# A gated linear attention with a gated feed-forward layer: the queries' factor from one reciprocal in place of a second scan

## The chip, the cores and the metric

The kernel runs on one core of one Trainium2 chip. The core has five engines that run side by side and wait for each other by semaphores: TensorE (PE, matrix products into PSUM; its weight loads are listed as PEld), VectorE (DVE), ScalarE (ACT), GpSimd (POOL) and SyncE (SP, which here issues nearly all DMAs). The metric is the device time of one execution in microseconds (us); lower is better. "Before" is the median of three runs.

## What is computed

For each of 4 x 8 heads, a state of 48 x 48 is carried along 768 positions. Each position scales the state's rows by a gate, adds an outer product of key and value, and reads the state with the query. All heads' results, 384 numbers for each of 3072 tokens, go through a feed-forward layer of width 2048:

```python
f = 1.0 / (1.0 + np.exp(-f_logit))
for t in range(S):
    state = f[:, :, t, :, None] * state + np.einsum('bhd,bhe->bhde', k[:, :, t], v[:, :, t])
    y[:, :, t] = np.einsum('bhd,bhde->bhe', q[:, :, t], state)
...
h = x @ w_in
g = h * np.clip(h + 3.0, 0.0, 6.0) / 6.0
return g @ w_out
```

## The kernel before

**Units.** The sequence is cut in chunks of 128 positions, 6 for each of 4 batches: 24 units, taken chunk by chunk through all batches (`UNITS`, line 40). A unit holds all 8 heads of its batch: 112 rows (two heads of 48 rows, at rows 0 and 64), 4 pairs of heads side by side, 128 positions each, so 512 elements in a row. Instead of stepping through positions, a unit multiplies keys and queries by factors made of the gates, and forms all pairs of positions by matrix products.

**The factors.** Let f be the gates of a chunk. `back` (line 349) scans them from the chunk's end to its start and makes `suffix`: at place t the product of the gates from t to the end, with 1 behind the last one. The tile has 4 x 129 elements, and one reset column for each pair of heads keeps the pairs apart. `kmul` (361) multiplies the key at t by the suffix product from t+1 on. `end` (368) keeps the whole chunk's product, which `decay` (381) applies to the carried state and which a check at the end of the program looks at: where a chunk's product is too small, the program computes everything again by a slow path. The queries need the reciprocal of the same suffix products. Before the change they come from a second scan: `rend` (turn, line 365) takes the reciprocal of the whole chunk's product, 4 elements in a row, into the reset columns of a tile that is otherwise zero, and `fwd` (forward, 373) scans the gates forward from there, 516 elements, in place over the gates. `qmul` (376) multiplies the queries by the result, one element further on.

**The rest of a unit.** `load` (330), `loadq` (333) and `loadv` (338) bring gates, queries with keys, and values; `gate` (343) is the sigmoid on ACT. `tk` and `ktok` transpose the keys, `att` (413) forms the scores, `mask` (423) applies causality on VectorE, `kv` (447) the chunk's own contribution to the state, `carry0` and `carry1` (466, 473) add it to the decayed state, `qs` (480) and `av` (496) give the result, and `xh`, `ym`, `xl`, `hole` (522 to 538) write it as a high and a low part into `xts`, the input of the feed-forward layer.

**The feed-forward layer.** A group is one chunk of all 4 batches, 512 tokens. For each of 16 slices of the width: `mm1` (line 560, nine matmuls, as weights and data are split into high and low parts and three products are kept), `relu` (570, ACT), `g` (574, VectorE), `gh` (583, ACT, the high part of the product), `gl` (587, VectorE, the low part) and `mm2` (604, nine matmuls; the last three read the low part). `pair` and `single` are PSUM banks 0 to 3 and 4; `tg` has three buffers, `gg` two. In the program's first part the weights are also converted from their 64-bit form, slice by slice: `ld`, `z`, `cy`, `mid`, `lim`, `dif`, `top`, `high`, `low` (lines 244 to 293) on ACT, VectorE and POOL.

**Order.** The order of all steps is written out by hand in `ORDER` (line 51), one token for each step and unit or slice. Each engine takes its own instructions in exactly that order; `ON_POOL` (43) names the steps that go to POOL instead of VectorE, some of the `kmul`, `qmul` and `decay` among them. A late instruction therefore delays everything behind it on its engine. Gates and suffix tiles have two buffers each (line 199), so the gate load of a unit waits for the `qmul` two units earlier.

Of the kernel before, what the change touches and what calls it, by code (L numbers as in the profile page):

```python
# [60 lines left out]
mid.3 rend.4 kmul.4 lowi.2 hole.3 ld.5 wd.2~hole.3 ga.1 lim.3 dif.3 back.5 mm2a.0 mm1a.2.1 mm2a.1 end.4 lim.4 end.5  # L61
z.4 mm1b.0.2 mm1b.1.0 mm1b.2.3 relub.0 relua.2 relub.1 top.3 fwd.4 qmul.4 cy.5 high.3 kmul.5 gb.0 ga.2 gb.1 tk.4.4
ktok.4 z.5 mm2b.0 tk.5.0 mm2a.2 ld.6~relub.0 mid.4 dif.4 top.4 mid.5 low.3 rend.5 high.4 relub.2 ktok.5 lim.5 low.4
fwd.5 dif.5 mm1.3.2 mm2b.1 att.4.0 mm1.4.4 cy.6 lim.6 mid.6 top.5 dif.6 decay.5 gb.2 mm2b.2 loadv.4~cy.5 ld.7
# [3 lines left out]
gh.5 mid.8 top.7 rend.6 dif.8 top.8 high.7 low.7 gl.5 fwd.6 tk.6.2 ktok.6 cy.9 high.8 low.8 mid.9 mm1.6.3 mm1.7.2  # L68
# [3 lines left out]
top.11 gl.8 decay.7 mm2.7 tk.7.3 mm2.8 low.10 carry0.6 xl.5 load.8 lim.12 relu.9 g.9 rend.7 carry1.6 ktok.7 z.12 ld.13  # L72
ld.14 cy.13 gh.9 fwd.7 mid.12 dif.12 top.12 gl.9 mm1.10.4 qs.6.2 kv.7.0 carry0.7 av.6 qmul.7 z.13 relu.10 xh.6 xl.6
# [4 lines left out]
rend.8 kmul.8 g.13 gh.12 gate.9 gl.12 end.8 relu.15 gh.13 mm2.12 tk.8.0 gl.13 back.9 fwd.8 mm2.13 gh.14 relu.16 ktok.8  # L78
g.15 qmul.8 kv.8.0 att.8.2 load.10 gh.15 kmul.9 decay.8 gl.14 rend.9 mm2.14 gl.15 mask.8 carry0.8 g.16 carry1.8 lowo.0
lowo.2 mm2.15 mm1.17.4 mm1.18.0 mm1.19.1 gh.16 gate.10 outs.0 outs.2 outv.1 fwd.9 gl.16 mm2.16 od.0 tk.9.3 od.2  # L80
relu.17 od.1 back.10 relu.18 end.9 end.10 qmul.9 g.17 rend.10 fwd.10 gh.17 relu.19 ktok.9 g.19 g.18 lowo.1 mm1.20.4
# [12 lines left out]
carry1.13 back.15 mask.13 mm1.33.4 mm2.30 qs.13.0 kv.14.2 av.13 hole.12 rend.15 loadq.15 loadv.15 load.16 loadv.16  # L94
loadq.16 gl.31 fwd.15 end.15 decay.15 qmul.15 kmul.15 carry0.14 relu.33 g.33 carry1.14 mm2.31 xh.13 xl.13 mm1.34.2
mm1.35.1 tk.15.3 outs.3 gate.16 gh.32 gl.32 back.16 rend.16 od.3 relu.34 gh.33 relu.35 end.16 outs.5 g.34 ktok.15
mm1.36.4 g.35 outv.4 od.5 kmul.16 att.14.2 kv.15.0 gl.33 od.4 relu.36 g.36 carry0.15 carry1.15 mask.14 fwd.16 qmul.16
# [60 lines left out]
def gla_moe(ctx: ExitStack, tc: tile.TileContext, unit, w, outT):  # L158
    nc = tc.nc
# [71 lines left out]
    rend = const.tile([PR, NP, C + 1], F32, name="rend")  # L231
    nc.gpsimd.memset(rend, 0.0)
# [88 lines left out]
    def engine(op, i):  # L321
        return nc.gpsimd if f"{op}.{i}" in ON_POOL else nc.vector

    def prep(i):
# [4 lines left out]

        def load():  # L330
            nc.sync.dma_start(out=gates[i % 2], in_=fg[u])
# [26 lines left out]
        def parts_of(t, x):
            return t[:, x].rearrange("r n c o t -> r c (n o) t")

        def kmul():
            t = chunks[i]
            engine("kmul", i).tensor_tensor(parts_of(t, 1), parts_of(t, 1), split(sf[:, :, 1:C + 1]), op=ALU.mult)  # L363

        def turn():
            nc.vector.reciprocal(rend[:, :, 0], sf[:, :, 0])
# [4 lines left out]
        past = gt[:, :NP * (C + 1)]

        def forward():
            nc.vector.tensor_tensor_scan(past, past, flat(rend), 0.0, op0=ALU.mult, op1=ALU.add)  # L374

        def qmul():
            t = chunks[i]
            to = past.rearrange("r (p c) -> r p c", p=NP)[:, :, 1:]
            engine("qmul", i).tensor_tensor(parts_of(t, 0), parts_of(t, 0), split(to), op=ALU.mult)  # L379

        def decay():
            engine("decay", i).tensor_tensor(
                decayed[i % 2][:, :, 0:D], state[b],
                ends[:, i].unsqueeze(2).broadcast_to([PR, NP, D]), op=ALU.mult,
            )
# [534 lines left out]
```

## Time and profile before

| | |
|---|---|
| median of 3 runs | 500.14 us (499.82 to 503.69) |
| span of the profiled execution | 500.6 us |
| HBM read, written | 36.43 MB, 4.72 MB |
| `back`, 24 scans on VectorE (L350) | 31.4 us busy |
| `qmul` on POOL (L379), 13 | 16.5 us busy, mean 1272 ns |
| `qmul` on VectorE (L379), 11 | 8.7 us busy, mean 797 ns |
| `rend` memset on POOL (L232) | 0.5 us, once, at 2.6 us |

The profile is of one execution; its times run from the first to the last instruction. A row of a timeline has the start in us, the duration in us, engine, line, operation, output and inputs, shapes and a count; in brackets the time that the engine was idle just before, and what ended that wait. A row of the groups by line has the count, then busy time in us and the mean of one in ns, then idle time before. [...] The 40 digits of an engine are its busy share, in tenths, in 40 equal slices of the span.

### The profile page before, as it was taken

What the parts mean: (1) busy time and instruction counts of PE and PEld (TensorE: products, weight loads), DVE (VectorE), ACT (ScalarE), POOL (GpSimd) and SP (SyncE); (2) the same over time, 40 slices, a digit from 0 to 9 for tenths busy, and PEclk for the clock granted to TensorE, in tenths of its full rate; (3) what the DMA queues carried; (4) which work ended last, traced back from release to release, by engine and by line L of the source; (5) the groups of instructions that cost most, each with busy time, mean ns of one, the idle gap of its engine ahead of it and who ended that gap; (6) DMA issues with size and microseconds to landing.
All of it is one profiled execution on the core that took longest, in us unless ns stands there. A gap on an engine that the chain in (4) does not pass through costs nothing.

```text
span 500.6 us, 11481 instructions
## 1 busy us (share of the span) xinstructions
PE 487.3 (97%) x4958; PEld 391.3 (78%) x4958; DVE 295.0 (59%) x462; ACT 217.6 (43%) x372; POOL 53.0 (11%) x57
## 2 busy tenths in 40 slices
PE   8789999999999999999999999999999999999996
PEld 4478787787888888788888888887887888788885
DVE  5959999989675736757405576645542243333341
ACT  5769989754343315433305434224322232333331
POOL 2211512203200200210100010100100000000000
PEclk9979999999999999999999999999999999999998
DMA  8877766432320330523100143300200000100001
GB/s 283 265 232 246 240 223 205 138 136 86 101 82 2 113 96 1 190 73 126 51 0 3 58 131 95 105 8 2 99 26 9 24 2 0 64 0 1 0 1 69
DMA packets 18969, 44.91 MB, mean 90 GB/s; under 512 B 2528, under 2 KB 8544, under 8 KB 18912
## 3 DMA queue, kind: packets, MB, share of 16 engines
q1 hardware_dynamic: 18768, 43.98, 26.5%
q8 instruction: 41, 0.67, 0.5%
q14 instruction: 16, 0.13, 0.1%
q10 hardware_dynamic: 144, 0.13, 0.1%
HBM read 36.43 MB, written 4.72 MB: 82 GB/s over the span
## 4 chain that ended last, share of the span: by engine, by line
PE 82%; DVE 11%; DMA 3%; ACT 1%; issue 1%; POOL 1%; SPq 0%; DVEq 0%; ACTq 0%
PE o L604 35%; PE pair L560 25%; PE single L560 11%; PE pair L487 2%; PE pair L456 2%; PE pair L504 2%; PE pair L418 2%; DVE top L281 2%; DMA raw<-w 2%; DVE w L285 1%; DVE gates L374 1%; DVE weight L293 1%; PE pair L655 1%; PE single L655 1%; DMA v<-unit 1%
## 5 line engine op out<-in xcount | busy, mean ns | idle before, releaser
L604 PE MATMUL o<-gg,weight 128*128 128x512 f32 x693 | 173.2, 399 | 0.5 <-DVE gg L587 0.5
L604 PEld LDWEIGHTS o<-gg,weight 128*128 128x128 f32 x693 | 128.0, 188 | 32.0 <-DVE gg L587 1.8
L560 PE MATMUL pair<-xts,weight 128*128 128x512 f32 x576 | 141.9, 396 | 0.0
L560 PEld LDWEIGHTS pair<-xts,weight 128*128 128x128 f32 x576 | 107.1, 188 | 24.5 <-DVE weight L293 0.2
L587 DVE TENSOR_TENSOR gg<-tg,gg 128x512 fp32r<-128x512 f32 x77 | 52.9, 692 | 68.2 <-ACT gg L583 68.2
L583 ACT ACTIVATE gg<-tg 128x512 fp32r<-128x512 f32 x77 | 48.2, 629 | 91.5 <-PE o L604 75.0
L574 DVE SCALAR_TENSOR_TENSOR tg<-tg,pair 128x512 f32<-128x512 f32 x64 | 42.8, 683 | 56.5 <-ACT tg L570 56.4
L570 ACT ACTIVATE tg<-pair,half 128x512 f32<-128x512 f32 x64 | 43.4, 685 | 62.9 <-PE pair L560 55.9
L560 PE MATMUL single<-xts,weight 128*128 128x512 f32 x261 | 66.5, 399 | 0.0
L560 PEld LDWEIGHTS single<-xts,weight 128*128 128x128 f32 x261 | 48.2, 188 | 10.9
L374 DVE TENSOR_TENSOR_SCAN gates<-gates,rend 112x516 f32<-112x516 f32 x24 | 33.3, 1386 | 0.2
L350 DVE TENSOR_TENSOR_SCAN suffix<-gates,unit 112x516 f32<-112x516 f32 x24 | 31.4, 1309 | 2.8 <-ACT gates L344 2.8
L570 ACT ACTIVATE tg<-single,half 128x512 f32<-128x512 f32 x29 | 19.8, 682 | 28.0 <-PE single L560 24.9
L363 POOL TENSOR_TENSOR qkf<-qkf,suffix 112x512 f32<-112x512 f32 x13 | 18.2, 1400 | 99.0 <-DVE suffix L350 35.2
L523 ACT ACTIVATE xts<-pair 112x512 fp32r<-112x512 f32 x24 | 14.3, 595 | 28.7 <-PE pair L456 14.6
L574 DVE SCALAR_TENSOR_TENSOR tg<-tg,single 128x512 f32<-128x512 f32 x29 | 19.7, 680 | 10.4 <-ACT tg L570 10.3
L604 PE MATMUL o<-xts,weight 128*128 128x512 f32 x96 | 25.3, 397 | 0.6 <-ACT xts L583 0.6
L379 POOL TENSOR_TENSOR qkf<-qkf,gates 112x512 f32<-112x512 f32 x13 | 16.5, 1272 | 85.0 <-DVE gates L374 40.6
L425 DVE TENSOR_TENSOR a<-pair,causal 128x512 f32<-128x512 f32 x24 | 16.4, 685 | 13.1 <-PE pair L504 9.3
L604 PEld LDWEIGHTS o<-xts,weight 128*128 128x128 f32 x96 | 17.8, 188 | 5.4 <-ACT xts L583 1.0
L456 PE MATMUL pair<-v,ktok 64*48 64x48 f32 (+1 forms) x768 | 16.4, 218 | 4.5 <-DVE top L281 2.4
L536 DVE TENSOR_TENSOR xts<-pair,xts 112x512 fp32r<-112x512 f32 x19 | 13.1, 687 | 11.6 <-ACT xts L523 11.6
(92 smaller groups left out, 452.2 us busy)
## 6 DMA issues: line engine op xcount, KB each, us to landing
qkf<-unit SPq DMA_DIRECT2D x24, 512.0 KB, 4.2
raw<-w SPq DMA_DIRECT2D x16, 768.0 KB, 5.5
gates<-unit SPq DMA_DIRECT2D x24, 258.5 KB, 3.2
v<-unit SPq DMA_DIRECT2D x24, 200.0 KB, 4.3
outT<-os SPq DMA_DIRECT2D x17, 256.0 KB, 2.1
xts<-xts SPq DMA_DIRECT2D x48, 48.0 KB, 2.2
weight<-w SPq DMA_DIRECT2D x3, 192.0 KB, 3.6
outT<-os SPq DMA_DIRECT2D x1, 128.0 KB, 3.7
```

The source lines that it names most:

```text
L350: nc.vector.tensor_tensor_scan(flat(sf)[:, ::-1], gt[:, 1:][:, ::-1], flat(unit)[:, ::-1], 0.0, op0=ALU.mult, op1=ALU.add,)
L363: engine("kmul", i).tensor_tensor(parts_of(t, 1), parts_of(t, 1), split(sf[:, :, 1:C + 1]), op=ALU.mult)
L374: nc.vector.tensor_tensor_scan(past, past, flat(rend), 0.0, op0=ALU.mult, op1=ALU.add)
L379: engine("qmul", i).tensor_tensor(parts_of(t, 0), parts_of(t, 0), split(to), op=ALU.mult)
L425: nc.vector.tensor_tensor(d["a"].rearrange("r p e t -> r e p t"), d["at"], causal.unsqueeze(1).unsqueeze(1).broadcast_to([128, 2, NP, HC]) ...
L456: nc.tensor.matmul(d["kv"][r:r + m, odd, c, n], d["ktok"][rs, 2 * n + part, r:r + m], heads_of(vt[rs], part, n, e)[:, :D], start=(odd, e) ...
L560: nc.tensor.matmul(h, win(f, a, k), g["xt"][:, k, :g["n"] // C, b], start=i == 0, stop=i == 3 * KT - 1,)
L570: nc.scalar.activation(d["t"], d["h"], AF.Relu, bias=half, scale=1.0 / 6.0)
L574: nc.vector.scalar_tensor_tensor(d["t"], d["t"], 1.0, d["h"], op0=ALU.min, op1=ALU.mult)
L583: nc.scalar.activation(d["gg"][:, 0], d["t"], AF.Copy)
L587: engine("gl", f if g["name"] == "0" else NU).tensor_tensor(d["gg"][:, 1], d["t"], d["gg"][:, 0].bitcast(F32), op=ALU.subtract)
L604: nc.tensor.matmul(g["o"][m], wout(f, a, m), g[f]["gg"][:, b], start=f == 0 and i == 0, stop=f == NF - 1 and i == 2, skip_group_check=True,)
```

## The change

`rend`, `fwd`, the tile of reset columns and its memset are taken out. In their place stands one step, `inv`: VectorE's reciprocal of the suffix products from the second column on, 4 x 128 elements in a row, written over the gates. `qmul` reads the gates' own columns in place of those one further on. In `ORDER` each `rend` token is dropped and each `inv` token stands where `fwd` stood; all other tokens keep their order.

```diff
@@ ORDER
-load.0 gate.0 back.0 rend.0 loadq.0 load.1 ld.0 loadv.0~gate.0 kmul.0 fwd.0 qmul.0 gate.1 warm.17 tk.0.3 ktok.0 warm.6
-att.0.0 kv.0.2 cy.0 back.1 loadq.1 loadq.2~load.1 mid.0 load.2 kmul.1 mask.0 rend.1 fwd.1 lim.0 qmul.1 ld.1 z.0
+load.0 gate.0 back.0 loadq.0 load.1 ld.0 loadv.0~gate.0 kmul.0 inv.0 qmul.0 gate.1 warm.17 tk.0.3 ktok.0 warm.6
+att.0.0 kv.0.2 cy.0 back.1 loadq.1 loadq.2~load.1 mid.0 load.2 kmul.1 mask.0 inv.1 lim.0 qmul.1 ld.1 z.0
...
@@
-    rend = const.tile([PR, NP, C + 1], F32, name="rend")
-    nc.gpsimd.memset(rend, 0.0)
@@
-        def turn():
-            nc.vector.reciprocal(rend[:, :, 0], sf[:, :, 0])
-
         def end():
             nc.scalar.activation(ends[:, i], sf[:, :, 0], AF.Copy)
 
-        past = gt[:, :NP * (C + 1)]
-
-        def forward():
-            nc.vector.tensor_tensor_scan(past, past, flat(rend), 0.0, op0=ALU.mult, op1=ALU.add)
+        def inverse():
+            nc.vector.reciprocal(rows, sf[:, :, 1:C + 1])
 
         def qmul():
             t = chunks[i]
-            to = past.rearrange("r (p c) -> r p c", p=NP)[:, :, 1:]
-            engine("qmul", i).tensor_tensor(parts_of(t, 0), parts_of(t, 0), split(to), op=ALU.mult)
+            engine("qmul", i).tensor_tensor(parts_of(t, 0), parts_of(t, 0), split(rows), op=ALU.mult)
@@
-            "kmul": kmul, "rend": turn, "end": end, "fwd": forward,
+            "kmul": kmul, "end": end, "inv": inverse,
```

More of the change, by code (lines that the diff above doesn't have):

```diff
@@ L60 @@
 load.5 ld.4~carry0.3 hole.2~wd.0 wd.1 loadq.5 relua.0 high.2 cy.3 xh.3 ym.3 ga.0 relua.1 xl.3 back.4 gate.5 z.3 cy.4
[L61 to L64, printed above, removed]
+mid.3 kmul.4 lowi.2 hole.3 ld.5 wd.2~hole.3 ga.1 lim.3 dif.3 back.5 mm2a.0 mm1a.2.1 mm2a.1 end.4 lim.4 end.5
+z.4 mm1b.0.2 mm1b.1.0 mm1b.2.3 relub.0 relua.2 relub.1 top.3 inv.4 qmul.4 cy.5 high.3 kmul.5 gb.0 ga.2 gb.1 tk.4.4
+ktok.4 z.5 mm2b.0 tk.5.0 mm2a.2 ld.6~relub.0 mid.4 dif.4 top.4 mid.5 low.3 high.4 relub.2 ktok.5 lim.5 low.4
+inv.5 dif.5 mm1.3.2 mm2b.1 att.4.0 mm1.4.4 cy.6 lim.6 mid.6 top.5 dif.6 decay.5 gb.2 mm2b.2 loadv.4~cy.5 ld.7
 loadv.5~ld.6 loadq.6~loadv.4 z.6 relu.3 top.6 high.5 cy.7 z.7 relu.4 g.3 low.5 decay.4 qmul.5 mask.4 kv.4.2 kv.5.0 g.4
@@ L67 @@
 ld.10 loadq.7~z.8 gl.3 back.6 mid.7 low.6 lim.7 att.5.2 av.4 kmul.6 g.5 mask.5 dif.7 gl.4 mm2.3 mm2.4 end.6 lim.8 z.9
-gh.5 mid.8 top.7 rend.6 dif.8 top.8 high.7 low.7 gl.5 fwd.6 tk.6.2 ktok.6 cy.9 high.8 low.8 mid.9 mm1.6.3 mm1.7.2
+gh.5 mid.8 top.7 dif.8 top.8 high.7 low.7 gl.5 inv.6 tk.6.2 ktok.6 cy.9 high.8 low.8 mid.9 mm1.6.3 mm1.7.2
 mm1.8.4 load.7~ld.10 ld.11 loadv.6 qmul.6 xh.4 ym.4 z.10 relu.6 g.6 relu.7 gh.6 xl.4 gate.7 g.7 lim.9 mm2.5 qs.5.0
@@ L71 @@
 kmul.7 dif.10 low.9 top.10 high.10 loadv.7 hole.4 ld.12 end.7 cy.12 gh.8 mm1.9.2 mid.11 lim.11 gl.7 dif.11 decay.6
-top.11 gl.8 decay.7 mm2.7 tk.7.3 mm2.8 low.10 carry0.6 xl.5 load.8 lim.12 relu.9 g.9 rend.7 carry1.6 ktok.7 z.12 ld.13
-ld.14 cy.13 gh.9 fwd.7 mid.12 dif.12 top.12 gl.9 mm1.10.4 qs.6.2 kv.7.0 carry0.7 av.6 qmul.7 z.13 relu.10 xh.6 xl.6
+top.11 gl.8 decay.7 mm2.7 tk.7.3 mm2.8 low.10 carry0.6 xl.5 load.8 lim.12 relu.9 g.9 carry1.6 ktok.7 z.12 ld.13
+ld.14 cy.13 gh.9 inv.7 mid.12 dif.12 top.12 gl.9 mm1.10.4 qs.6.2 kv.7.0 carry0.7 av.6 qmul.7 z.13 relu.10 xh.6 xl.6
 carry1.7 mm2.9 att.7.2 qs.7.0 mid.13 g.10 high.11 cy.14 gate.8 low.11 gh.10 z.14 lim.14 high.12 hole.6 ld.15 load.9
@@ L77 @@
 lim.15 dif.15 top.15 low.14 mm2.11 high.15 relu.12 low.15 mm1.14.0 mm1.15.1 mm1.16.4 back.8 g.12 relu.13 relu.14 g.14
[L78 to L81, printed above, removed]
+kmul.8 g.13 gh.12 gate.9 gl.12 end.8 relu.15 gh.13 mm2.12 tk.8.0 gl.13 back.9 inv.8 mm2.13 gh.14 relu.16 ktok.8
@@ L82 @@
+g.15 qmul.8 kv.8.0 att.8.2 load.10 gh.15 kmul.9 decay.8 gl.14 mm2.14 gl.15 mask.8 carry0.8 g.16 carry1.8 lowo.0
+lowo.2 mm2.15 mm1.17.4 mm1.18.0 mm1.19.1 gh.16 gate.10 outs.0 outs.2 outv.1 inv.9 gl.16 mm2.16 od.0 tk.9.3 od.2
+relu.17 od.1 back.10 relu.18 end.9 end.10 qmul.9 g.17 inv.10 gh.17 relu.19 ktok.9 g.19 g.18 lowo.1 mm1.20.4
 qs.8.0 att.9.2 av.8 kmul.10 qmul.10 decay.9 decay.10 mask.9 gl.17 kv.9.0 mm2.17 tk.10.2 mm1.21.3 xh.8 gh.18 load.11
 loadq.11 load.12 loadv.10 gh.19 gl.18 carry0.9 carry1.9 gl.19 xl.8 mm2.18 ktok.10 gate.11 relu.20 relu.21 back.11 g.21
-g.20 qs.9.0 att.10.2 av.9 kv.10.0 mm2.19 mm1.22.4 gate.12 back.12 end.12 end.11 gh.20 rend.11 carry0.10 fwd.11 qmul.11
@@ L85 @@
-load.13 loadq.12 kmul.11 mask.10 gl.20 tk.11.2 mm2.20 loadv.11 xh.9 relu.22 rend.12 g.22 gh.21 ktok.11 gh.22 gl.21
-gl.22 decay.11 fwd.12 carry1.10 mm1.23.4 relu.23 g.23 kmul.12 gate.13 mm2.21 mm1.24.3 gh.23 relu.24 mm2.22 mm1.25.4
+g.20 qs.9.0 att.10.2 av.9 kv.10.0 mm2.19 mm1.22.4 gate.12 back.12 end.12 end.11 gh.20 carry0.10 inv.11 qmul.11
+load.13 loadq.12 kmul.11 mask.10 gl.20 tk.11.2 mm2.20 loadv.11 xh.9 relu.22 g.22 gh.21 ktok.11 gh.22 gl.21
+gl.22 decay.11 inv.12 carry1.10 mm1.23.4 relu.23 g.23 kmul.12 gate.13 mm2.21 mm1.24.3 gh.23 relu.24 mm2.22 mm1.25.4
@@ L87 @@
 qmul.12 gl.23 relu.25 xl.9 g.24 gh.24 qs.10.0 att.11.2 av.10 kv.11.0 xh.10 mask.11 back.13 carry0.11 xl.10 g.25
-rend.13 carry1.11 mm2.23 mm1.26.3 tk.12.2 mm1.27.4 ktok.12 relu.26 gl.24 fwd.13 g.26 qs.11.0 att.12.2 av.11 hole.10
+carry1.11 mm2.23 mm1.26.3 tk.12.2 mm1.27.4 ktok.12 relu.26 gl.24 inv.13 g.26 qs.11.0 att.12.2 av.11 hole.10
 load.14 loadv.12 kv.12.0 loadq.13 loadv.13 qmul.13 mask.12 decay.12 gh.25 xh.11 gate.14 relu.27 xl.11 back.14
-carry0.12 rend.14 carry1.12 gl.25 mm2.24 hole.11 hole.9 load.15 gh.26 fwd.14 gl.26 g.27 hole.8 loadv.14 loadq.14
+carry0.12 carry1.12 gl.25 mm2.24 hole.11 hole.9 load.15 gh.26 inv.14 gl.26 g.27 hole.8 loadv.14 loadq.14
@@ L93 @@
 tk.14.4 g.32 qs.12.0 att.13.2 av.12 kv.13.0 qmul.14 end.14 ktok.14 gate.15 xh.12 gh.31 decay.14 carry0.13 xl.12
[L94 to L97, printed above, removed]
+carry1.13 back.15 mask.13 mm1.33.4 mm2.30 qs.13.0 kv.14.2 av.13 hole.12 loadq.15 loadv.15 load.16 loadv.16
+loadq.16 gl.31 inv.15 end.15 decay.15 qmul.15 kmul.15 carry0.14 relu.33 g.33 carry1.14 mm2.31 xh.13 xl.13 mm1.34.2
+mm1.35.1 tk.15.3 outs.3 gate.16 gh.32 gl.32 back.16 od.3 relu.34 gh.33 relu.35 end.16 outs.5 g.34 ktok.15
+mm1.36.4 g.35 outv.4 od.5 kmul.16 att.14.2 kv.15.0 gl.33 od.4 relu.36 g.36 carry0.15 carry1.15 mask.14 inv.16 qmul.16
 mm2.32 mm2.33 tk.16.4 gh.34 gh.35 ktok.16 qs.14.2 att.15.0 av.14 kv.16.2 decay.16 gl.35 carry0.16 carry1.16 mask.15
```

17 lines of the change are left out of this document (8 added, 9 removed).

## The prediction, made before the changed kernel ran

> **What bounds the kernel now.** I read the page's head first, then the groups by line with the shapes kept apart, then busy time by stage, and then the timeline of single instructions around each of the 24 places of the new instruction.
>
> ```profile
> span 500.6 us, 11481 instructions
> PE 487.3 (97%) x4958; PEld 391.3 (78%) x4958; DVE 295.0 (59%) x462; ACT 217.6 (43%) x372; POOL 53.0 (11%) x57
> DVE  5959999989675736757405576645542243333341
> ...
> 20.00:34.30 14.30, 10.55 (x261) 8.78 (x256) 8.86 (x13) 8.70 (x19) 2.49 (x2) 0.76 0.83 270
> 34.30:91.00 56.70, 55.92 (x699) 45.67 (x698) 55.84 (x91) 49.55 (x76) 14.51 (x9) 1.00 0.62 211
> 91.00:135.00 44.00, 43.98 (x456) 34.95 (x457) 37.65 (x57) 22.64 (x39) 9.93 (x8) 1.00 0.35 112
> 135.00:360.00 225.00, 225.00 (x2385) 182.70 (x2384) 129.01 (x202) 80.39 (x148) 20.81 (x19) 1.00 0.22 70
> ```
>
> Over the whole span TensorE is the bound: 487.3 of 500.6 us. The stages differ, and the last four rows show it (their columns are the stretch, busy time of PE, weight loads, DVE, ACT, POOL, then the granted clock and the DMA). Up to 34.3 us nothing is full but the DMA (0.83). From 34.3 to 91 us VectorE is busy 55.84 of 56.70 us, and TensorE 55.92: both are full, and VectorE has no spare time. From 135 to 360 us it has 96 us to spare. So the price of a VectorE instruction depends on its place: in full before 91 us, and later only what the lead of TensorE's inputs does not cover.
>
> **The price of the new instruction.** Removed are 24 scans of 516 elements (L374), 24 reciprocals of 4 elements (L366) and one POOL memset at 2.6 us, which stands in front of nothing late. Added are 24 reciprocals of 512 elements. The 512-element one isn't in the trace; the 4-element one is.
>
> ```profile
> L374 DVE TENSOR_TENSOR_SCAN gates<-gates,rend 112x516 f32<-112x516 f32 x24 | 33.3, 1386 | 0.2
> L366 DVE RECIPROCAL rend<-suffix 112x4 f32<-112x4 f32 x24 | 4.2, 175 | 0.2
> L425 DVE TENSOR_TENSOR a<-pair,causal 128x512 f32<-128x512 f32 x24 | 16.4, 685 | 13.1 <-PE pair L504 9.3 <-ACT th L631 3.7
> L478 DVE TENSOR_TENSOR state<-pair,middle 112x192 f32<-112x192 f32 x16 | 5.5, 350 | 0.1
> ...
> 22.68 0.35 DVE L269 TENSOR_SCALAR top<-top 128x768 uint16<-128x768 uint16 x1
> 22.95 1.22 DVE L374 TENSOR_TENSOR_SCAN gates<-gates,rend 112x516 f32<-112x516 f32 x1
> 24.09 0.53 DVE L281 TENSOR_TENSOR top<-top,mid 128x768 int16<-128x768 uint16 x1
> ```
>
> From 192 to 512 elements a product grows by 335 ns, 1.05 ns an element, which leaves about 150 ns that every instruction has. A reciprocal of 4 takes 175 ns, 25 ns over that. Counted over four elements that is 6 ns each; counted over the three steps from the first to the last element it is 8.3 ns. For 512 elements that gives 3.3 to 4.4 us of duration. From start to start an undisturbed instruction takes some 0.08 us less than its duration (the scan at 22.95 lasts 1.22, the next starts after 1.14). I take 4.3 us from start to start, the count by steps, since the common 150 ns holds the first element already. The bounds are 4.5 us above, and below the 0.6 us of a 512-element product. What goes is 1.14 + 0.09, so a place costs 3.1 us more; where the scan was stretched beyond 1.22, that much less. Over 24 places it is at most 74 us of VectorE time.
>
> [...]
>
> The rest of the edit is cheap. qmul reads the same tile at another offset, 512 elements as before. The order of all other steps is kept, so nothing is moved past a queue; but everything behind an inv on VectorE comes 3.1 us later, and so do POOL's qmuls, attention's scores, and the gate load two units on, which waits on SP for qmul to free the gates tile.
>
> **Stage by stage.** Units 0 to 3, up to 34.3 us:
>
> ```profile
> 7.75 0.69 DVE L379 TENSOR_TENSOR qkf<-qkf,gates 112x512 f32<-112x512 f32 x1
> 8.47 0.33 SPq L331 DMA_DIRECT2D gates<-unit  x1
> ...
> 24.65 1.07 PE L456 MATMUL pair<-v,ktok 64*64 64x48 f32 x48 [2.40 <-DVE top L281]
> ...
> 27.82 0.36 DVE L276 TENSOR_SCALAR mid<-top 128x768 uint16<-128x768 uint16 x1 [1.61 <-ACT top L267]
> ...
> 34.31 0.69 DVE L425 TENSOR_TENSOR a<-pair,causal 128x512 f32<-128x512 f32 x1 [3.71 <-ACT th L631]
> ```
>
> The load at 8.47 us is issued when qmul.0 ends (8.44), so unit 0's 3.1 us delay the whole SP queue; unit 1's second gate load slides by 4 us in the same way. Against that, four places add 12.4 us to VectorE, but it idles 1.61 and 3.71 us here, and TensorE 2.40 us for a v load that is late by less than VectorE is. Walking the four units through by these rows, the step at 34.31 us comes about 4.5 us later. Bounds: 2 (the load alone) and 8 (12.4 less the larger idle times).
>
> Units 4 to 7, 34.3 to 91 us:
>
> ```profile
> 41.01 2.24 DVE L374 TENSOR_TENSOR_SCAN gates<-gates,rend 112x516 f32<-112x516 f32 x1
> ...
> 90.28 0.69 DVE L587 TENSOR_TENSOR gg<-tg,gg 128x512 fp32r<-128x512 f32 x1
> ...
> 91.02 0.97 PE L604 MATMUL o<-gg,weight 128*128 128x512 f32 x3 [0.49 <-DVE gg L587]
> ```
>
> Unit 4's scan was stretched by 1.0, so it costs 2.1, the other three 3.1 each: 11.4 us. The cover is the stage's idle VectorE time, 56.70 - 55.84 = 0.9. At 91.02 TensorE waits for VectorE already, so no lead is left there: +10.5 us.
>
> Units 8 to 10, to 135 us:
>
> ```profile
> 116.58 4.68 PE L604 MATMUL o<-gg,weight 128*128 128x512 f32 x18
> 117.46 0.68 DVE L587 TENSOR_TENSOR gg<-tg,gg 128x512 fp32r<-128x512 f32 x1
> ...
> 132.62 0.36 DVE L382 TENSOR_TENSOR decayed<-state,ends 112x192 f32<-112x192 f32 x1 [2.36 <-PE pair L487]
> 133.84 0.69 DVE L425 TENSOR_TENSOR a<-pair,causal 128x512 f32<-128x512 f32 x1 [0.86 <-PE pair L504]
> 134.45 0.68 DVE L587 TENSOR_TENSOR gg<-tg,gg 128x512 fp32r<-128x512 f32 x1
> ...
> 134.09 2.37 PE L604 MATMUL o<-gg,weight 128*128 128x512 f32 x9
> ...
> 138.95 2.11 PE o L604 x9
> ```
>
> A second matmul block (L604) takes 2.11 us, and reads the low half of gg in its last three of nine matmuls, 1.4 us after its start. At 116.58 two blocks take 4.68 instead of 4.22, held by the low half that ends at 118.14: no lead, so unit 8 costs 3.1. Units 9 and 10 add 6.2; VectorE's idle 2.36 and 0.86 take 3.2 of it, and the low half that ends at 135.13 has 0.4 us until 135.5: +2.6. Stage: +5.7 us.
>
> Units 11 to 23, after 135 us, where each delay meets idle VectorE time soon:
>
> ```profile
> 146.47 0.68 DVE L587 TENSOR_TENSOR gg<-tg,gg 128x512 fp32r<-128x512 f32 x1
> ...
> 147.61 2.34 PE L604 MATMUL o<-gg,weight 128*128 128x512 f32 x9
> ...
> 154.85 0.69 DVE L587 TENSOR_TENSOR gg<-tg,gg 128x512 fp32r<-128x512 f32 x1 [0.31 <-ACT gg L583]
> ...
> 156.07 2.26 PE L604 MATMUL o<-gg,weight 128*128 128x512 f32 x9
> ...
> 233.87 0.69 DVE L587 TENSOR_TENSOR gg<-tg,gg 128x512 fp32r<-128x512 f32 x1 [2.38 <-ACT gg L583]
> 239.30 0.67 DVE L574 SCALAR_TENSOR_TENSOR tg<-tg,pair 128x512 f32<-128x512 f32 x1
> ...
> 241.07 2.34 PE L560 MATMUL pair<-xts,weight 128*128 128x512 f32 x9
> ...
> 299.16 1.82 DVE L374 TENSOR_TENSOR_SCAN gates<-gates,rend 112x516 f32<-112x516 f32 x1
> 302.36 0.67 DVE L574 SCALAR_TENSOR_TENSOR tg<-tg,pair 128x512 f32<-128x512 f32 x1
> ...
> 305.09 0.36 PE L437 MATMUL pair<-ident,qkf 112*128 112x112 f32 x2
> ```
>
> Unit 11: the low half ends at 147.15 and is needed at 149.0, a lead of 1.9, so 1.2 is lost. Unit 12: 3.1 - 0.31 idle - 1.9 lead = 0.9. Units 17 and 18 stand close together: 3.1 - 2.38 + 3.1 = 3.8 late at 239.30, whose bank (0) the block at 241.07 overwrites 1.1 us after it is read: 2.7. Units 19 and 20: 3.1 + 2.5 (that scan took 0.6 more than 1.22) = 5.6 at 302.36; the transposes of unit 20 want the same bank 2.05 us after it: 3.5. The others meet idle times of 2 us and more, or a lead of about 3; I give them 0.6 together. Stage: +8.9 us, between 4 (leads twice as long) and 18.
>
> One thing more: the clock. The row from 20 to 34.3 us has a granted clock of 0.76 after TensorE's one long idle time (2.40 us), which is 0.24 x 14.3 = 3.4 us of TensorE work. The new stalls of 2.7, 3.1 and 3.5 us are as long. Before 135 us such a loss mostly runs beside VectorE's own lateness; I count one in full: +3.4, bounds 0 and 10.
>
> [...]
>
> **Sum:** 4.5 + 10.5 + 5.7 + 8.9 + 3.4 = 33.0 us on the span of 500.6, which is 0.5 above the median of 500.14: 533 us. Its own range, from the bounds of the terms, is 515 to 553.
>
> **Rivals.** (1) Later delays aren't absorbed. ACT runs relu and the high halves in one order, so a late product can hold the relu behind it, and the lead of two gg buffers is used up at each place. Then all 13 late units cost 3.1: 500 + 4.5 + 10.5 + 9.3 + 40.3 = 565 us. It decides once a delay outlasts the next relu. Against it:
>
> ```profile
> ACT gg L583 <- PE o L604: 75.0, 35, 11.9
> ```
>
> ACT waits 75 us in 35 places for TensorE, which is lead to give away. [...] (3) Not slower: the 25 ns are a fixed start-up of the reciprocal, and elements then stream like a product's, 0.6 us each. VectorE then gains 0.6 in each place. Only the seven places between 34.3 and 135 us where it holds TensorE count: 500 - 4 = 496 us. It decides if the instruction takes under 1.2 us. The 25 ns allow it, but then every other kind of instruction's 150 ns would not hold for this one.
>
> **How the numbers follow.** Forecast 0.70, rival 1 0.12, rival 2 0.12, rival 3 0.06. The range runs from rival 2's 504 to 556, where the forecast's range ends with some room, and leaves out rivals 1 and 3: 0.18. A measurement tells about 1%, 5 us, from no change: faster takes a sixth of rival 3, 0.01; same the rest of it and some of rival 2, 0.08; slower 0.91.
>
> **What will show it.** [...] VectorE's busy time should rise by about 70 us to 365. The step that stood at 91.02 us should come near 106; the last block before 135 us near 156. After that TensorE's waits on VectorE should lie at units 11, 12, 17/18 and 19/20, not at every unit; if they lie at all 13, rival 1 holds. The clock row should show one or two more stretches at half speed.

## The result, and the profile after

The changed kernel takes 516.54 us (median of 4 runs, 513.95 to 517.27) against 501.91 us (4 runs, 499.82 to 505.34): a ratio of 1.0292 [1.0252, 1.0332]. It is slower, as forecast, but the loss of some 15 us is less than half of the 33 us that the sum gave. A span is some 1.7 us shorter than the time of the same run. The profiled execution has a span of 515.6 us, 15.0 more than the 500.6 of before. In the changed kernel's profile the lines have moved: the new reciprocal is L366, `qmul` L370, `kmul` L360, `mask` L416, `tk` L428, `g` L565, `gl` L578, `mm1` L551, `mm2` L595.

The head of the page and its costliest groups, changed kernel:

```profile
span 515.6 us, 11453 instructions
...
PE 491.7 (95%) x4958; PEld 393.7 (76%) x4958; DVE 337.6 (65%) x438; ACT 218.1 (42%) x372; POOL 51.0 (10%) x56
...
DVE  6999999988978784877823369746852343333342
...
L366 DVE RECIPROCAL gates<-suffix 112x512 f32<-112x512 f32 x24 | 80.2, 3341 | 0.0
L347 DVE TENSOR_TENSOR_SCAN suffix<-gates,unit 112x516 f32<-112x516 f32 x24 | 30.9, 1289 | 2.8 <-ACT gates L341 2.8
```

The new instruction takes 3.34 us each time, not 4.4. VectorE's busy time rises by 42.6 us (295.0 to 337.6), not by 70. The groups account for it: 80.2 came, the scans' 33.3 and the small reciprocals' 4.2 went, and that makes 42.7. The digits of VectorE at the left end have risen from "59599999" to "69999999": the holes that it had in the first stage are filled.

Busy time by stage, changed kernel (columns as before: the stretch, PE, weight loads, DVE, ACT, POOL, then the granted clock and the DMA):

```profile
0.00:20.00 20.00, 16.77 (x250) 9.30 (x250) 15.53 (x17) 11.35 (x19) 4.80 (x18) 0.83 0.74 259
20.00:34.30 14.30, 11.09 (x292) 8.47 (x285) 14.27 (x15) 9.82 (x22) 1.58 (x3) 0.88 0.73 241
34.30:91.00 56.70, 52.77 (x587) 42.83 (x588) 55.00 (x80) 45.54 (x71) 13.68 (x9) 0.97 0.62 209
91.00:135.00 44.00, 40.70 (x402) 31.84 (x401) 40.40 (x52) 23.30 (x37) 6.87 (x5) 0.96 0.34 114
135.00:360.00 225.00, 220.47 (x2380) 178.78 (x2379) 151.03 (x185) 78.65 (x145) 22.35 (x21) 1.00 0.22 70
```

From 20 to 34.3 us VectorE was busy for 8.86 us and now is for 14.27: the stage swallowed the new work. From 34.3 to 135 us TensorE was busy for 99.9 of 100.7 us and now for 93.5. There the loss shows.

To see where the time goes, I take four instructions of VectorE that both kernels have, one at the end of each stage, and subtract their starts. Each start is a row of the two timelines. In the changed kernel the first, third and fourth are:

```profile
34.37 0.68 DVE L416 TENSOR_TENSOR a<-pair,causal 128x512 f32<-128x512 f32 x1
...
145.85 0.68 DVE L578 TENSOR_TENSOR gg<-tg,gg 128x512 fp32r<-128x512 f32 x1
...
375.39 0.69 DVE L659 COPY os<-o 128x512 f32<-128x512 f32 x1 [0.53 <-PE o L595]
```

The last of them in the old kernel:

```profile
360.04 0.69 DVE L668 COPY os<-o 128x512 f32<-128x512 f32 x1 [2.67 <-PE o L604]
```

| VectorE instruction | start before, us | later by, us | added in the stage, us |
|---|---|---|---|
| `mask.3` | 34.31 | 0.06 | 0.06 |
| `gl` ahead of the block at 91.02 | 90.28 | 7.95 | 7.9 |
| last `gl` ahead of 135 us | 134.45 | 11.40 | 3.45 |
| first copy of the last outputs | 360.04 | 15.35 | 3.95 |

One trace of the old kernel is not a sharp ruler. Two kernels of the next section have the same instructions up to `mask.3` and start it at 32.79 and 31.77 us. So the change adds 0.1 to 2.6 us in the first stage, and the 0.06 of the table is the lower end. From there on the second of them stays 1.9 us ahead of this trace (88.33 and 132.59 us for the next two rows).

The `gl` that stood at 90.28 us, and the block that waits for it, in the timeline of the changed kernel:

```profile
92.20 3.33 DVE L366 RECIPROCAL gates<-suffix 112x512 f32<-112x512 f32 x1
...
95.46 0.28 DVE L273 TENSOR_SCALAR mid<-top 128x768 uint16<-128x768 uint16 x1
...
98.23 0.68 DVE L578 TENSOR_TENSOR gg<-tg,gg 128x512 fp32r<-128x512 f32 x1
...
98.96 0.96 PE L595 MATMUL o<-gg,weight 128*128 128x512 f32 x3 [2.43 <-DVE gg L578]
```

From the reciprocal's start to the next instruction's are 95.46 - 92.20 = 3.26 us. The scan and the small reciprocal that went took 1.14 + 0.09 = 1.23, so a place costs 2.03 us more, not 3.1. The block that stood at 91.02 stands at 98.96, and its wait has grown from 0.49 to 2.43 us.

TensorE's longest waits, changed kernel (us in total, times, longest):

```profile
PE pair L409 <- DVE qkf L370: 3.9, 2, 2.1
PE o L595 <- DVE gg L578: 3.5, 2, 2.4
PE pair L428 <- DVE a L416: 1.3, 1, 1.3
PE pair L478 <- ACT xts L525: 1.2, 1, 1.2
PE o L631 <- DVE th L626: 1.2, 1, 1.2
...
PE single L551 <- DVE weight L290: 0.8, 1, 0.8
PE pair L447 <- DVE tg L565: 0.8, 1, 0.8
...
PE pair L551 <- DVE tg L565: 0.8, 1, 0.8
```

The two waits of the first row are attention's scores of units 0 and 2 behind `qmul`. They stand in the first stage, whose end isn't late in these two traces. The third row is new, and the prediction did not name it:

```profile
154.76 3.34 DVE L366 RECIPROCAL gates<-suffix 112x512 f32<-112x512 f32 x1
158.13 0.69 DVE L370 TENSOR_TENSOR qkf<-qkf,gates 112x512 f32<-112x512 f32 x1
158.74 0.68 DVE L360 TENSOR_TENSOR qkf<-qkf,suffix 112x512 f32<-112x512 f32 x1
...
159.34 0.68 DVE L416 TENSOR_TENSOR a<-pair,causal 128x512 f32<-128x512 f32 x1
...
160.09 0.60 PE L428 MATMUL pair<-ident,qkf 112*128 112x112 f32 x4 [1.29 <-DVE a L416]
```

This is unit 11. Its `kmul` and the mask of unit 10 stand behind `inv` and `qmul` on VectorE. The transposes of unit 11's keys (L428) need both: the keys, which `kmul` has ready at 159.42 us, and PSUM bank 2, where unit 10's scores stay until the mask has read them at 160.02 (`att.10.2` and `tk.11.2` in `ORDER`). The mask ends last, and TensorE waits 1.29 us for it, before the product that the prediction looked at.

### The profile page after: what moved, and what is told of

It reads as the page before. It is cut to its first block, busy times and chain, and to the rows that moved or that the text cites. A ratio compares the mean times of both kernels' runs of the same rounds, so it can differ in the third digit from the quotient of the medians.

```text
span 515.6 us, 11453 instructions
## 1 busy us (share of the span) xinstructions
PE 491.7 (95%) x4958; PEld 393.7 (76%) x4958; DVE 337.6 (65%) x438; ACT 218.1 (42%) x372; POOL 51.0 (10%) x56
## 4 chain that ended last, share of the span: by engine, by line
PE 64%; DVE 8%; ACT 1%; issue 1%; DMA 1%; ACTq 0%
PE o L595 28%; PE pair L551 20%; PE single L551 7%; DVE gates L366 4%; PE pair L478 2%; PE pair L409 2%; PE pair L495 1%; PE pair L646 1%; PE single L646 1%; DVE suffix L347 1%; PE pair L447 1%; DVE tg L565 1%; DMA gates<-unit 1%; PE pair L428 1%; DVE qkf L360 0%
## 5 line engine op out<-in xcount | busy, mean ns | idle before, releaser
L595 PE MATMUL o<-gg,weight 128*128 128x512 f32 x693 | 170.9, 396 | 3.5 <-DVE gg L578 3.5
L595 PEld LDWEIGHTS o<-gg,weight 128*128 128x128 f32 x693 | 127.9, 188 | 33.1 <-DVE gg L578 4.9
L551 PE MATMUL pair<-xts,weight 128*128 128x512 f32 x576 | 142.4, 397 | 1.2 <-DVE tg L565 0.8
L551 PEld LDWEIGHTS pair<-xts,weight 128*128 128x128 f32 x576 | 106.9, 188 | 26.7 <-DVE tg L565 1.0
L578 DVE TENSOR_TENSOR gg<-tg,gg 128x512 fp32r<-128x512 f32 x77 | 53.4, 698 | 57.0 <-ACT gg L574 56.9
L574 ACT ACTIVATE gg<-tg 128x512 fp32r<-128x512 f32 x77 | 48.3, 629 | 99.9 <-PE o L595 74.4
L366 DVE RECIPROCAL gates<-suffix 112x512 f32<-112x512 f32 x24 | 80.2, 3341 | 0.0
L565 DVE SCALAR_TENSOR_TENSOR tg<-tg,pair 128x512 f32<-128x512 f32 x64 | 42.4, 680 | 52.3 <-ACT tg L561 52.1
L551 PE MATMUL single<-xts,weight 128*128 128x512 f32 x261 | 68.0, 404 | 0.9 <-DVE weight L290 0.8
L551 PEld LDWEIGHTS single<-xts,weight 128*128 128x128 f32 x261 | 48.7, 191 | 12.7 <-DVE weight L290 1.3
L360 POOL TENSOR_TENSOR qkf<-qkf,suffix 112x512 f32<-112x512 f32 x13 | 17.2, 1326 | 100.7 <-DVE suffix L347 68.9
L370 POOL TENSOR_TENSOR qkf<-qkf,gates 112x512 f32<-112x512 f32 x13 | 16.7, 1288 | 99.8 <-DVE gates L366 59.5
L565 DVE SCALAR_TENSOR_TENSOR tg<-tg,single 128x512 f32<-128x512 f32 x29 | 19.7, 679 | 10.4 <-ACT tg L561 10.4
L595 PE MATMUL o<-xts,weight 128*128 128x512 f32 x96 | 25.4, 397 | 0.6 <-ACT xts L574 0.6
L595 PEld LDWEIGHTS o<-xts,weight 128*128 128x128 f32 x96 | 17.8, 188 | 5.5 <-ACT xts L574 1.0
L416 DVE TENSOR_TENSOR a<-pair,causal 128x512 f32<-128x512 f32 x24 | 16.3, 681 | 7.2 <-PE pair L495 6.6
L527 DVE TENSOR_TENSOR xts<-pair,xts 112x512 fp32r<-112x512 f32 x19 | 13.0, 684 | 11.5 <-ACT xts L514 11.5
L409 PE MATMUL pair<-qkf 48*64 48x64 f32 x768 | 16.5, 222 | 3.9 <-DVE qkf L370 3.9
```

What stands on the lines that cost most here:

```text
L366: nc.vector.reciprocal(rows, sf[:, :, 1:C + 1])
L409: nc.tensor.matmul(d["at"][HC * odd:HC * (odd + 1), e, 2 * n + c], t[rs, 1, n, c, odd], t[rs, 0, n, c, odd], start=True, stop=True,)
L416: nc.vector.tensor_tensor(d["a"].rearrange("r p e t -> r e p t"), d["at"], causal.unsqueeze(1).unsqueeze(1).broadcast_to([128, 2, NP, HC]) ...
L551: nc.tensor.matmul(h, win(f, a, k), g["xt"][:, k, :g["n"] // C, b], start=i == 0, stop=i == 3 * KT - 1,)
L565: nc.vector.scalar_tensor_tensor(d["t"], d["t"], 1.0, d["h"], op0=ALU.min, op1=ALU.mult)
L574: nc.scalar.activation(d["gg"][:, 0], d["t"], AF.Copy)
```

## The experiments

Three questions were open: whether the stages really lose what the lag table says, or the loss comes from interplay; whether the forecast's walk through the stages was right and its price alone wrong; and what the half clock, which shows in the windows above (0.83, 0.88), costs. All kernels use the changed kernel's or the old kernel's text with one edit. The kernels of the first two groups were compared with the old kernel on the same chip, at a median of 500.95 us (17 runs) for the first four and of 501.25 us (6 runs) for the next four; the last two with 502.22 us (17 runs).

**The reciprocal in some units alone.** Three kernels keep the second scan except in one range of units:

```diff
+            if i in [0, 1, 2, 3]:
+                to = rows
...
-warm.1 ym.1 mask.2 kmul.3 rend.3 lowi.0 lim.1 fwd.3 dif.1 qmul.3
+warm.1 ym.1 mask.2 kmul.3 lowi.0 lim.1 inv.3 dif.1 qmul.3
```

> The reciprocal in units 0 to 3 alone, the scan in the other 20. Theory A (up to 34 us the loads' landing sets the end, so VectorE's extra 2.0 us a place is absorbed): 0 to +1.5 us on before, and the mask of unit 3 starts within 1 us of its 34.3 us in before. Theory B (a delay of the first units is carried to the end, and the trace of the full change hides it behind a lucky clock): +3 to +6 us.

> The reciprocal in units 4 to 10 alone. Theory A (VectorE has no idle time from 34 to 130 us, so each place costs its 2.0 us nearly in full): +10 to +13 us on before, most of the full change's loss. Theory B (the loss is spread evenly over the 24 places, 0.6 us each): +4 us.

> The reciprocal in units 11 to 23 alone. Theory A (VectorE's idle time absorbs most): +2 to +5 us on before, in two or three places, at units 11/12 and where two inv stand close together (19 and 20). Theory B (evenly spread): +8 us.

| reciprocal in units | median, us | ratio | span, us |
|---|---|---|---|
| 0 to 3 | 503.28 (10 runs) | 1.0046 [1.0020, 1.0071] | 502.0 |
| 4 to 10 | 511.92 (4 runs) | 1.0225 [1.0165, 1.0286] | 510.7 |
| 11 to 23 | 506.08 (8 runs) | 1.0113 [1.0081, 1.0144] | 503.3 |

By medians these are +2.3, +11.0 and +5.1 us. The second lies where theory A put it and the third at A's upper end of 5; B's 4 and 8 us lie outside their intervals. The first lies between A and B, with an interval from 1.0 to 3.6 us: a part of what the first four places delay does come out later. Its trace shows that only in part (its `mask.3` is 0.14 us late, its `gl` of the old 90.28 us 1.68), as the old trace's own `mask.3` is 1.5 and 2.5 us later than those of the second and third kernel. The three sum to 18.4 us and the full change has about 15; with the widths of the four intervals this difference isn't clear of noise. The third kernel, with no reciprocal before unit 11, has the same new wait of the transposes in its waits of TensorE:

```profile
PE pair L442 <- DVE a L430: 1.3, 1, 1.3
```

**The price, set by idle work.** Three kernels keep the scan and add, between it and `qmul`, memsets of columns that are zero already. They hold up VectorE as a longer reciprocal would, at a price that their number sets. They don't hold up the 13 `qmul` that run on GpSimd, which wait for the scan alone: that of unit 6 starts 1.36 us behind the start of the scan, without memsets and with three, and 3.43 us behind the start of the reciprocal.

```diff
+        def pad():
+            for _ in range(4):
+                nc.vector.memset(rend[:, :, 1:], 0.0)
```

> The kernel before with four VectorE memsets of 512 zeros behind each fwd, in the zero part of the reset tile (some 0.5 us each by the 516-element one of before, so about 2.0 us more a place, as the reciprocal). Theory A (VectorE's time alone counts): the time of the full change within 3 us, 512 to 518 us. Theory C (something of the reciprocal itself costs: how it reads, or who waits for its result): well below that, under 508 us.

> The scan with three memsets of 512 zeros behind it. Four of them took 2.52 us from start to start instead of the 2.0 expected (each waits for the one ahead, 0.66 us apiece), so three cost 1.86 us a place, a little less than the reciprocal's 2.03. Theory A (only VectorE's time a place counts): 9 to 14 us on before, a little under the full change. Theory C (the reciprocal is special, and memsets cost more for the same time): 18 us or more, three quarters of what four memsets cost.

> The scan with five memsets behind it: 3.18 us a place, the price that the prediction gave the reciprocal (3.1). Theory P (the walk through the stages was right and only the price was wrong): the predicted 33 us on before, between 29 and 40. Theory Q (the walk overstates by itself: the loss is proportional to the price, as 15 us at 2.03 say): 23 to 25 us.

The first rows of the timeline of the kernel with five, at unit 0, show what price that makes:

```profile
6.49 1.23 DVE L374 TENSOR_TENSOR_SCAN gates<-gates,rend 112x516 f32<-112x516 f32 x1
7.89 0.48 DVE L378 MEMSET rend<- 112x512 f32 x1 [0.17 <-DVE gates L374]
8.55 0.48 DVE L378 MEMSET rend<- 112x512 f32 x1 [0.17 <-DVE rend L378]
...
10.93 0.63 DVE L383 TENSOR_TENSOR qkf<-qkf,gates 112x512 f32<-112x512 f32 x1
```

`qmul` starts 4.44 us after the scan instead of 1.26 (6.49 to 7.75 before): 3.18 us a place, the price that the prediction had assumed. Memsets of one tile wait for each other, 0.66 us from start to start. So four of them cost 2.52 us (more than the 4 x 0.485 of their durations), and three 1.86. That is why the kernel with four, which was meant to cost 2.0 us a place, takes 526.36 us and fits neither of its two expectations.

| memsets | us a place | median, us | ratio | span, less 500.6 |
|---|---|---|---|---|
| 3 | 1.86 | 513.31 (4 runs) | 1.0225 [1.0186, 1.0263] | 12.0 |
| the change | 2.03 | 516.54 (4 runs) | 1.0292 [1.0252, 1.0332] | 15.0 |
| 4 | 2.52 | 526.36 (4 runs) | 1.0503 [1.0443, 1.0563] | 24.8 |
| 5 | 3.18 | 543.22 (4 runs) | 1.0839 [1.0792, 1.0885] | 38.0 |

The change lies between three and four memsets, as its price does, so most of what it does to the time is what any instruction of that length on VectorE would do in these places. Counted over all places the order is the same: the change takes 42.6 us of VectorE, three memsets 36.4 (318.9 - 295.0 busy and 12.5 waiting for each other or the scan), and four 51.1. A remainder of a few us stays open, since memsets are not a neutral stand-in: with three, the `kmul` and `qmul` on VectorE take 14.4 us instead of 17.5, and GpSimd's `qmul` comes earlier than in the change. Three memsets cost 12 us, inside theory A's 9 to 14.

At five the loss is 38 us by the span of the profiled execution, the fastest of the four, and 42 by the medians. Theory Q (23 to 25) falls. P's 29 to 40 holds the first figure and not the second. The loss is not proportional to the price. From 1.86 to 3.18 us a place it grows by 26 us by the spans, which is 19.7 us for each us of price, and read back along that slope it is zero at 1.25 us a place. Not all of this growth is VectorE's time: the mean granted clock of TensorE is 0.989 in the profiled execution with three memsets and 0.969 in the one with five, which has 0.94 from 34.3 to 91 us and 0.98 from 135 to 360.

Where the cover lies, the same table of starts shows for all of them (later than in the old kernel's trace by, us):

| | `mask.3` | `gl` at 90.28 | `gl` at 134.45 | copy at 360.04 |
|---|---|---|---|---|
| 3 memsets | 0.72 | 6.16 | 8.06 | 12.23 |
| the change | 0.06 | 7.95 | 11.40 | 15.35 |
| 4 memsets | 2.13 | 9.26 | 15.87 | 24.95 |
| 5 memsets | 4.77 | 16.41 | 22.84 | 38.34 |

From four to five memsets the first stage becomes 2.64 us longer, which is 4 x 0.66: from there each added microsecond is paid in full. With five, four places add 12.7 us and 4.8 arrive, and with four 10.1 and 2.1: measured from this trace of the old kernel the stage covers 8 us, out of the 10.7 us that VectorE idles up to 34.3 us in it (34.3 - 14.77 - 8.86). Measured from the start of `mask.3` at 31.77 us it covers 2.5 less. The change adds less than the 8.1 us of four full prices, since two of the scans that it replaces were stretched (2.01 us in unit 1, 1.41 in unit 2): VectorE's busy time up to 34.3 us rises by 6.2 us. Little of it arrives, 0.1 to 2.6 us.

**The reciprocal in two halves.** Two reciprocals of 256 elements in place of one of 512:

```diff
-            nc.vector.reciprocal(rows, sf[:, :, 1:C + 1])
+            for p in (0, 2):
+                nc.vector.reciprocal(rows[:, p:p + 2], sf[:, p:p + 2, 1:C + 1])
```

> Each reciprocal as two instructions of 256 elements a row. If an element costs 6.25 ns and an instruction 0.14 us beside them (as 3341 ns for 512 says with the common fixed part), each half takes 1.74 us, and the pair 0.1 us more a place than the whole: 1 to 3 us slower than the full change. If the price has another form (a start-up of a microsecond or more), the halves take clearly more than 1.8 us each and the kernel is 10 us or more slower than the full change.

It takes 518.43 us (4 runs), 1.0323 [1.0276, 1.0371]. The group of the halves:

```profile
L378 DVE RECIPROCAL gates<-suffix 112x256 f32<-112x256 f32 x48 | 80.5, 1719 | 0.0
```

From 256 to 512 elements the duration grows by 3341 - 1719 = 1622 ns, which is 6.3 ns an element, and about 0.1 us is fixed. A half takes 1.72 us, as the first form of the price says (1.74), and that settles the price law for these sizes. The median is some 2 us above the full change's, as expected too, but the intervals overlap and the reason given doesn't hold: a pair takes 3.27 us from start to start (12.35 to 15.62 in unit 1), 0.01 more than the whole and not 0.1, and VectorE's busy time is 338.3 us for 337.6.

**The reciprocal on another engine.** GpSimd raises the suffix products to the power of -1:

```diff
-            nc.vector.reciprocal(rows, sf[:, :, 1:C + 1])
+            nc.gpsimd.tensor_tensor(rows, sf[:, :, 1:C + 1], neg.unsqueeze(2).broadcast_to([PR, NP, C]), op=ALU.pow)
```

> The reciprocal as a power of -1 on GpSimd, 24 instructions of 512 elements, none on VectorE. VectorE is rid of 1.23 us a place, which by theory A is worth 5 to 8 us in units 4 to 10, if POOL takes 3 us or less each: 493 to 497 us. If POOL takes 5 us or more each, attention's scores and POOL's own kmul wait for it in every unit: slower than before by 10 us or more.

```profile
L379 POOL TENSOR_TENSOR gates<-suffix,neg 112x512 f32<-112x512 f32 x24 | 1968.2, 82011 | 54.7 <-DVE suffix L352 36.6 <-issue 11.5 <-ACT xts L530 6.7
```

One run: 2265.67 us. At 82 us apiece this is no way to take the work off VectorE.

**The half clock.** In the changed kernel TensorE's clock is halved in four stretches while it works: from 11.5 to 18.3, 25.1 to 28.6, 35.4 to 38.8 and 100.2 to 103.6 us (granted clock 0.50 or 0.51 in each). The last, in the windows of the changed kernel:

```profile
98.00:99.00 1.00, 0.04 (x1) 0.04 (x1) 1.00 (x3) 0.63 (x1) 0.00 (x0) 1.00 0.00 0
...
100.20:101.90 1.70, 1.70 (x62) 1.58 (x53) 1.70 (x4) 0.73 (x2) 0.00 (x0) 0.51 0.24 59
101.90:103.60 1.70, 1.70 (x5) 1.31 (x6) 1.70 (x4) 1.70 (x3) 0.00 (x0) 0.50 0.27 55
```

It begins 1.2 us after the wait of 2.43 us has ended, lasts 3.4 us and costs 1.7 us of TensorE work. In two kernels idle matmuls (`warm`, on a blank tile) fill the waits of the first stage: one is the old kernel with eight more, one the changed kernel with fourteen more.

```diff
-warm.1 ym.1 mask.2 kmul.3 rend.3 lowi.0 lim.1 fwd.3 dif.1 qmul.3 warm.1 kv.2.0
+warm.1 ym.1 mask.2 kmul.3 rend.3 lowi.0 lim.1 fwd.3 dif.1 qmul.3 warm.9 kv.2.0
```

> The kernel before, with eight more idle matmuls on TensorE ahead of unit 2's kv, where it waits 2.40 us for a value load and the granted clock falls to one half from 27.0 to 33.8 us. Theory W (that half clock sets the end of the first stage): 1.5 to 3 us faster, with a clock of 1.00 in the stretch from 20 to 34.3 us. Theory N (the loads' landing sets it): within 1 us of before.

> The full change, with eight and six more idle matmuls in TensorE's two waits of the first stage (2.07 us at 10.5, 1.78 us at 24.4). Theory W: 1 to 2.5 us faster than the full change, clock 1.00 up to 34.3 us. Theory N: within 1 us of the full change, so 14 to 16 us on before.

The stage from 20 to 34.3 us, first of the old kernel with eight more, then of the changed kernel with fourteen more:

```profile
20.00:34.30 14.30, 11.34 (x271) 8.52 (x264) 11.43 (x20) 10.07 (x20) 2.60 (x2) 1.00 0.77 259
```

```profile
20.00:34.30 14.30, 10.93 (x304) 8.02 (x304) 14.27 (x15) 9.66 (x21) 2.27 (x3) 1.00 0.80 262
```

Both run at the full clock there (1.00, from 0.76 and 0.88). The old kernel so takes 500.51 us (12 runs), 0.9967 [0.9938, 0.9997]: some 1.7 us less than without, on the same chip (theory W, though the interval reaches from 0.2 to 3.1 us), by something that has nothing to do with the change. The changed kernel takes 517.13 us (6 runs), 1.0292 [1.0258, 1.0325], the same as without, as theory N has it. Its span is 515.3 us for 515.6, although the first three stretches are gone, which had halved the clock for 13.7 us: VectorE is busy for 14.27 of the stage's 14.30 us and is its bound now, and a slower TensorE beside it costs nothing that these runs can show. Their intervals are 1.7 and 2 us wide to either side, so a cost of 1 or 2 us would not show.

## Why the prediction was right or wrong

**The step that failed is the price**, in the sentence "I take 4.3 us from start to start, the count by steps, since the common 150 ns holds the first element already". It measured 3.26 us from start to start, and 3.34 in duration. The 150 ns came from a line through 192 and 512 elements, and such a line counts every element, the first too; what it leaves holds none. The four-element instruction had to be counted the same way: 25 ns over four elements are 6.25 ns each, 512 of them 3.20 us, and with the 150 ns 3.35. That count stood in the prediction as the lower of the two, and I took the other one. The measured 3341 ns decide for the lower one.

**The walk through the stages held in sum, and not in every term.** The same walk with 2.03 us in place of 3.1, and nothing else changed, against the starts of the traces:

| term | forecast at 3.1 us | the same walk at 2.03 | the change | 5 memsets (3.18) |
|---|---|---|---|---|
| units 0 to 3 | 4.5 | 8.1 - 7.9 = 0.2 | 0.06 | 4.8 |
| units 4 to 7 | 10.5 | 8.1 - 1.0 - 0.9 = 6.2 | 7.9 | 11.6 |
| units 8 to 10 | 5.7 | 2.0 + 4.1 - 3.2 - 0.4 = 2.5 | 3.45 | 6.4 |
| units 11 to 23 | 8.9 | 3.1 | 3.95 | 15.5 |
| clock | 3.4 | 3.4 | in the rows above | in the rows above |
| sum | 33.0 | 15.4 | 15.4 | 38.3 |

7.9 is what the forecast's walk had covered in the first stage (12.4 less 4.5); the memsets show 5.5 to 8. In the fourth row unit 11 has 2.03 - 1.9 = 0.1, unit 12 nothing, units 17 and 18 2.03 - 1.1 = 0.9 (the idle 2.38 us covers the first of them whole), units 19 and 20 2.03 + 1.43 - 2.05 = 1.4, and the others the same 0.6. That the two sums meet is in part luck, as the stages below show: the clock is put too high, and unit 11 too low. At its own price, which the five memsets set, the forecast of 33 falls short, by 5 us by the span and 9 by the medians. So it was the price that made the forecast too high, and the rest of the walk errs a little to the other side. The price counts more than in proportion, since the covers are taken off first: a third less in the price makes more than half less in the sum. The lower end of the sum's own range, 515 us, does not follow from the bounds that it lists (2 + 10.5 + 5.7 + 4 + 0 = 22.2, which is 522 us), so that 516.54 us lies within it proves nothing.

**Stage by stage.** *Units 0 to 3:* the delays fill VectorE's idle time, as foreseen, and at the forecast's price 4.8 us or more arrive, within its bounds. The scores' waits of 2.07 us (unit 0) and 1.78 us (unit 2) are inside the stage. That the late loads of values are part of this stage's cover is likely but was not tried. *Units 4 to 7:* VectorE was full, as read, and the price arrived whole. Of the 1.7 us that came beyond the walk about 1 goes with the half clock from 35.4 to 38.8 us: the changed kernel with more idle matmuls, which has the full clock there, comes from `mask.3` to this `gl` in 62.75 us (33.85 to 96.60) and the changed kernel in 63.86 (34.37 to 98.23). The rest isn't settled. *Units 8 to 10:* the size came, but not at the place that the walk named. TensorE waits for no low half there. It waits for PSUM banks that `g` reads, and this `g` stands directly behind a reciprocal on VectorE (at 122.00 us in unit 8, at 138.88 in unit 10):

```profile
124.81 0.31 PE L447 MATMUL pair<-v,ktok 64*64 64x48 f32 x4
125.93 0.66 PE L447 MATMUL pair<-v,ktok 64*64 64x48 f32 x28 [0.81 <-DVE tg L565]
...
143.50 0.46 PE L478 MATMUL pair<-qkf,decayed 48*64 48x64 f32 x16 [0.69 <-DVE tg L565]
```

By the starts of what follows they make TensorE 1.3 and 0.7 us later, 2.0 in all; the rest of the 3.45 goes with the clock's term. *Units 11 to 23:* TensorE's waits on VectorE lie at few units, as foreseen: 17 and 18 with 0.78 us and 19 and 20 with 0.81 and 0.49, besides one of 0.46 at 218.9 us. Those of 19 and 20, in the timeline of the changed kernel:

```profile
314.95 3.35 DVE L366 RECIPROCAL gates<-suffix 112x512 f32<-112x512 f32 x1
...
319.35 1.28 DVE L565 SCALAR_TENSOR_TENSOR tg<-tg,pair 128x512 f32<-128x512 f32 x2
320.14 0.39 PE L428 MATMUL pair<-ident,qkf 112*128 112x112 f32 x2 [0.81 <-issue]
...
323.12 0.46 PE L478 MATMUL pair<-qkf,decayed 48*64 48x64 f32 x16 [0.49 <-ACT ktok L435]
```

The transposes of unit 20 start 0.1 us after the first of the two late `g` has ended. The profile names no releaser, but that fits the prediction's walk, by which they wait for the bank that this `g` reads; the product behind them waits for their copy. Unit 11 lost 1.29 us where the walk at 2.03 gives 0.1, at the transposes of its keys and not at the low half: there, too, the walk looked at the wrong consumer of VectorE. Unit 12 lost nothing.

**The clock.** A fall came, but behind the new wait of 2.43 us in units 4 to 7, and not behind one of the stalls of 2.7, 3.1 and 3.5 us that the prediction had named. The stretch is 3.4 us long (granted clock 0.50 to 0.51) and not 6.8 (27.0 to 33.8 us, 0.50) as after the old kernel's one long idle time of 2.40 us. Some 1.4 us of it arrive, less than half of the term: the block behind the wait starts 7.94 us later than in the old kernel (98.96 for 91.02), and unit 8's `kv` 9.38 later (124.81 for 115.43), with no wait of TensorE between them. What the other three stretches cost is less clear. The stretch at 35.4 us delays its stage by about 1 us, but the changed kernel with more idle matmuls, which lacks all three, isn't measurably faster.

**The rivals.** Rival 1 (later delays aren't absorbed) falls: 13 late places at 2.03 us would be 26 us after 135 us, and 3.95 came; with five memsets they would be 41 and 15.5 came. Rivals 2 and 3, in which the reciprocal takes 2.2 or 0.6 us, fall by the group's mean of 3341 ns.

## What to carry to other kernels

A price read from a small instance of an instruction has to be split into a fixed part and a part for each element in the same way as the line that gives the fixed part: if the line counts every element, so must the small instance. When a price is uncertain, redo the whole walk at each of its ends rather than scale the sum, since every stage takes its cover off first: here a loss of 12 us at 1.86 us a place became 38 us or more at 3.18. And name for each late instruction all that its engine holds behind it; the first consumer on the engine that sets the end is the one that counts, and in unit 11 it was a transpose of keys, in units 8 to 10 a product that waited for a bank, not the product that came to mind. Last, where a stage's end is read from one trace, look for other traces with the same instructions up to there: here three of them lie 2.5 us apart, where the table has 0.06 us for the change.

## What the runs showed of the hardware

The minimum, median and maximum durations of the two instructions in the changed kernel, in the trace's view of the tile `suffix`:

```profile
L347 DVE TENSOR_TENSOR_SCAN suffix<-gates,unit x24: 1220/1225/2230, 4.5 to 360.2; 112x516 f32<-112x516 f32 x24
L366 DVE RECIPROCAL gates<-suffix x24: 3327/3343/3349, 6.4 to 368.4; 112x512 f32<-112x512 f32 x24
```

In the old kernel's trace a scan of 516 elements lasts up to 1 us longer where it starts while an instruction of GpSimd is running: eight of the 48 scans do, and take 1.41 to 2.24 us, where the other 40 take 1.21 to 1.26. One beside which GpSimd began later (the scan at 201.60 us, GpSimd at 202.34) took 1.23. The reciprocal varies by 22 ns in 24 places, although six of them ran beside 0.5 to 1.4 us of GpSimd's work, which in four cases had begun first. Where it replaced a stretched scan, it cost that much less. A power on GpSimd takes 82.0 us for 112 x 512 elements. Memsets on VectorE that write the same tile start 0.66 us apart for 0.48 us of work.
